# Loading the first chunk's later weight columns in four pieces, and spreading T4 between the bank sums, in a fused GeGLU kernel

One core of a Trainium2 chip. The metric is the device time of one execution in microseconds (us), as the median over executions; the profile's span is about 1.8 us shorter than the time of the same run.

## The reference

```python
B, S, D, F = 1, 2048, 1024, 3584          # all bf16
def reference(x, w_gate, w_up, w_down):
    return (gelu_tanh(x @ w_gate) * (x @ w_up)) @ w_down
```

## The kernel before

The rows of x are taken in two halves of 1024, each as two token blocks of 512. The products with gate (j = 0) and up (j = 1) go by pairs of 128-column blocks, four blocks (two pairs) to a chunk of weights. From the second pair on a pair is computed with seven products of half size in place of eight (the Strassen-Winograd scheme): sums S1 to S4 of weight blocks (fp32r, by GpSimd, here called POOL, or VectorE, DVE) and sums T1 to T4 of blocks of x (by VectorE) are multiplied, and the partial results are summed in the PSUM banks. The T sums of x are made once, the S sums for every pair. The first pair is done plainly, since nothing is ready yet, and the second is where the scheme starts: it needs all of x, all T sums and its own S sums at once. The change touches only this start.

The loads, in program order:

```python
for kd in range(KH, KD):                       # KD = 8 blocks of D, KH = 4
    load_xT(xT, 0, 0, kd, kd + 1)              # transposing load on SyncE
    if kd == KH + 1:
        for j in range(2):
            load_w(first, j, 5, KD, act, 0, FA)    # last rows of the first columns
for j in range(2):
    load_w(first, j, 0, KD, sp, FA, FG)        # the later columns (second pair)
for k0 in range(0, KD, KH):
    load_xT(xT, 0, 1, k0, k0 + KH)             # x of the second token block
new_chunk((0, 1))
for j in range(2):
    load_w((0, 1), j, 0, KD)
```

The second pair, from the sums on (cuts marked):

```python
for j in range(2):                 # in the main part, after the first pair
    s_sum(0, first_pair, j, "s1")  # on GpSimd
    s_sum(0, first_pair, j, "s3")
s_sum(0, first_pair, 0, "s2", True)   # True: on VectorE
s_sum(0, first_pair, 0, "s4", True)
t_sum("t1")
pair_quads(hT, 0, first_pair, (0, PPG), {}, 0)   # m1 and m2 of the second pair
# ... a22, b22 on ScalarE; s2 of j = 1, t2 on VectorE
# ... first pair for the second token block, with t3 in it
s_sum(0, first_pair, 1, "s4", True)
t_sum("t4", 0, KH // 2)

# in pair_quads, after m5 and m6:
for j in range(2):
    add_m5(QB[j], QB[j])           # bank sums Q0, Q1
    prep(j, "s2")
done("m5")                         # here: late_t4, the second half of T4
for j in range(2):
    mm(RB[j], j, s(j, "s3"), tsum["t3"], False)   # m7
    add_m5(V_[j], RB[j])           # bank sums V0, V1
    # ... gelu, mult
# ... m3 with S4, m4 with T4

def late_t4():
    t_sum("t4", KH // 2, KH)
    last_on["t4"] = last_on["dve"]
def late_s():                      # the third pair's sums, on GpSimd
    last_on["pool_wait"] = last_on["t4"]   # ... wait for the last piece of T4
    for name in S_NAMES:           # s1, s2, s3, s4, a22
        for j in range(2):
            s_sum(0, PPG, j, name)
then = {"m5": [late_t4], "m4": [late_s]}
```

In the third pair the products follow as m1, m5 of j = 0, m6, m5 of j = 1, m7, m3, m4 (in the pairs after it m6 comes ahead of m5); m2 of a pair comes after m1 of the next. m5 reads S1 and T1, m6 S2 and T2, m7 S3 and T3, m3 S4. "Third pair" and "fourth pair" below count from one.

## Time and profile before

| | before |
|---|---|
| time, median of 6 runs | 541.53 us (541.3 to 541.9, and one run of 3140 us that the median counts; 541.34 without it) |
| span of the profiled run | 539.7 us |
| TensorE busy | 534.5 us |
| TensorE stops up to 33 us, by distance of starts | 1.53 us |
| TensorE starts the third pair / the fourth pair's first fp32r product | 33.80 / 47.91 us |

How to read it: once the fourth pair has started, TensorE never waits again in this profile, so the start of the fourth pair tells what the first 48 us cost. Lines of the profile are from the timeline (start, length, engine, line, operation, tiles, shapes, count; PE is TensorE's matmuls, PEld its weight loads).

```profile
33.80 1.90 PE L389 MATMUL bank<-xT,w_mem 128*128 128x512 bf16 x8
...
39.04 2.30 POOL L360 TENSOR_TENSOR s_mem<-w_mem,s_mem 128x512 fp32r<-128x512 bf16 x2
...
47.91 2.42 PE L389 MATMUL bank<-t_mem,s_mem 128*128 128x512 f32 x9
```

The second line is the two S4 of the third pair, over at 41.34; the weight load that reads the second of them (the 29th of the 40 products from 35.35) starts at 41.69, so GpSimd has 0.35 us to spare there.

### The profile page before, as it was taken

The numbers are of one execution on the slowest core, as the hardware profiler recorded it, in microseconds if no ns is written. First come the engines' busy times: TensorE is split into PE (matmuls) and PEld (weight loads), VectorE is DVE, ScalarE is ACT, GpSimd is POOL, SyncE is SP. The second block draws the span as 40 slices with busy tenths as digits, with TensorE's granted clock in tenths as the row PEclk, the third lists the DMA queues.
The fourth block names the chain that finished last, engine by engine and source line by source line (L and its number), as shares of the span: only waits on it lengthen the run. The fifth ranks groups of instructions, "written<-read, shape, count | busy, mean of one in ns | idle before, by whom it ended". The sixth has DMA issues, their size and how long they took to land.

```text
span 539.7 us, 7117 instructions
## 1 busy us (share of the span) xinstructions
PE 534.5 (99%) x2384; PEld 377.1 (70%) x2384; DVE 362.2 (67%) x475; ACT 263.3 (49%) x446; POOL 239.5 (44%) x210
## 2 busy tenths in 40 slices
PE   8999999999999999999999999999999999999997
PEld 3577777666776676767776677777777766866865
DVE  0978777787875997889574434444444469969951
ACT  1555555555555319216465555555555551452270
POOL 1369877777776000000056776666777730000000
PEclk9999999999999999999999999999999999999999
DMA  9927687695827876789950404041331466677846
GB/s 231 310 84 215 203 247 227 198 274 185 286 77 252 296 244 223 257 265 314 319 187 1 156 1 157 9 147 55 102 110 48 157 199 218 229 242 242 288 147 209
DMA packets 84772, 102.70 MB, mean 190 GB/s; under 512 B 18688, under 2 KB 66304, under 8 KB 84736
## 3 DMA queue, kind: packets, MB, share of 16 engines
q1 hardware_dynamic: 61936, 80.30, 46.2%
q10 hardware_dynamic: 22800, 21.96, 13.2%
q8 instruction: 19, 0.31, 0.2%
q14 instruction: 17, 0.14, 0.1%
HBM read 85.98 MB, written 12.58 MB: 183 GB/s over the span
## 4 chain that ended last, share of the span: by engine, by line
PE 93%; SPq 2%; DVE 1%; issue 1%; DMA 1%; ACT 0%; ACTq 0%; DVEq 0%
PE bank L389 61%; PE bank L664 33%; SPq L172 2%; DMA xT<-in_x_dram 1%; SPq L161 0%; DVE hT L277 0%; DVE t_mem L245 0%; DVE bank L412 0%; DVE s_mem L358 0%; DVE t_mem L239 0%; ACT o_sb L717 0%; SPq L167 0%; ACTq L717 0%; DVEq L239 0%
## 5 line engine op out<-in xcount | busy, mean ns | idle before, releaser
L389 PE MATMUL bank<-t_mem,s_mem 128*128 128x512 f32 x1056 | 249.7, 394 | 0.2 <-DVE bank L412 0.2
L389 PEld LDWEIGHTS bank<-t_mem,s_mem 128*128 128x128 f32 x1056 | 198.2, 188 | 44.3 <-DVE bank L412 0.9
L360 POOL TENSOR_TENSOR s_mem<-w_mem 128x512 fp32r<-128x512 bf16 x104 | 121.9, 1195 | 196.8 <-DVE t_mem L245 116.2
L277 DVE TENSOR_TENSOR hT<-w_mem,bank 128x512 bf16<-128x512 f32 x104 | 71.2, 686 | 86.6 <-PE bank L389 46.2
L664 PE MATMUL bank<-t_mem,s_mem 128*128 128x512 f32 x544 | 127.2, 392 | 0.0
L664 PEld LDWEIGHTS bank<-t_mem,s_mem 128*128 128x128 f32 x544 | 102.1, 188 | 22.2
L412 DVE TENSOR_TENSOR bank<-bank,m 128x512 f32<-128x512 f32 x108 | 69.8, 693 | 44.9 <-ACT m L434 42.7
L389 PE MATMUL bank<-xT,w_mem 128*128 128x512 bf16 x432 | 98.1, 380 | 0.2 <-DMA w_mem<-in_w_up_dram 0.2
L272 ACT ACTIVATE w_mem<-bank 128x512 f32<-128x512 f32 x104 | 61.8, 596 | 54.0 <-DVE bank L412 36.3
L389 PEld LDWEIGHTS <-w_mem 128*128 128x128 bf16 x432 | 40.1, 98 | 52.1 <-issue 6.8
L574 DVE TENSOR_TENSOR t_mem<-w_mem 128x1024 fp32r<-128x1024 bf16 x56 | 65.6, 1217 | 0.0
L360 POOL TENSOR_TENSOR s_mem<-w_mem,s_mem 128x512 fp32r<-128x512 bf16 x50 | 62.2, 1268 | 0.0
L360 POOL TENSOR_TENSOR s_mem<-s_mem,w_mem 128x512 fp32r<-128x512 f32 x50 | 58.0, 1180 | 0.0
L439 ACT COPY bank<-bank 128x512 f32<-128x512 f32 x54 | 30.8, 570 | 39.0 <-PE bank L389 38.5
L373 ACT CAST s_mem<-w_mem 128x512 fp32r<-128x512 bf16 x54 | 33.0, 615 | 30.5 <-PE bank L389 29.2
L639 DVE TENSOR_TENSOR s_mem<-hT 128x512 fp32r<-128x512 bf16 x52 | 34.2, 685 | 10.2 <-PE bank L664 9.4
L434 ACT COPY m<-bank 128x512 f32<-128x512 f32 x54 | 31.7, 587 | 18.4 <-PE bank L389 18.3
L664 PEld LDWEIGHTS <-hT 128*128 128x128 bf16 x224 | 21.2, 98 | 26.7 <-issue 2.1
L444 ACT COPY bank<-bank 128x512 f32<-128x512 f32 x54 | 30.8, 570 | 12.8 <-PE bank L389 12.8
L717 ACT CAST o_sb<-bank 128x512 bf16<-128x512 f32 x28 | 15.3, 585 | 39.6 <-PE bank L664 39.6
L599 DVE TENSOR_TENSOR o_sb<-wd_sb,o_sb 128x512 fp32r<-128x512 bf16 x28 | 31.4, 1121 | 0.5
L571 ACT CAST t_mem<-w_mem 128x1024 fp32r<-128x1024 bf16 x28 | 26.9, 1047 | 0.0
(44 smaller groups left out, 235.7 us busy)
## 6 DMA issues: line engine op xcount, KB each, us to landing
t_mem<-t_dram SPq DMA_DIRECT2D x56, 512.0 KB, 5.4
w_mem<-in_w_gate_dram ACTq DMA_DIRECT2D x10, 1024.0 KB, 5.6
w_mem<-in_w_up_dram ACTq DMA_DIRECT2D x10, 1024.0 KB, 8.7
wd_sb<-in_w_down_dram SPq DMA_DIRECT2D x28, 256.0 KB, 5.0
t_dram<-o_sb SPq DMA_DIRECT2D x28, 256.0 KB, 2.4
wd_sb<-in_w_down_dram SPq DMA_DIRECT2D x12, 512.0 KB, 8.4
w_mem<-in_w_down_dram SPq DMA_DIRECT2D x10, 512.0 KB, 5.8
w_mem<-in_w_down_dram SPq DMA_DIRECT2D x4, 1024.0 KB, 6.3
```

Of the source, the lines that this page charges most:

```text
L272: act(nc.scalar.activation(out=g_sb, in_=ps[:], func=ACT.Gelu_apprx_tanh))
L277: nc.vector.tensor_tensor(out=hT[:, fc, tb * TB : (tb + 1) * TB], in0=g_sb, in1=ps[:], op=ALU.mult,)
L360: pool(nc.gpsimd.tensor_tensor(out=t, in0=in0, in1=in1, op=op))
L373: act(nc.scalar.copy(out=t, in_=a(1, 1)))
L389: nc.tensor.matmul(banks[bank][:], lhsT=lhs[:, c, :], rhs=rhs[:, c, :], start=start and c == 0, stop=c == KH - 1, skip_group_check=True,)
L412: nc.vector.tensor_tensor(out=banks[dst][:], in0=banks[src][:], in1=m5[j][:], op=ALU.add)
L434: act(nc.scalar.copy(out=m5[j][:], in_=banks[V_[j]][:]))
L439: act(nc.scalar.copy(out=banks[RB[j]][:], in_=banks[QB[j]][:]))
L574: dve(nc.vector.tensor_tensor(out=t, in0=in0, in1=in1, op=ALU.subtract))
L599: dve(nc.vector.tensor_tensor(out=t, in0=in0, in1=in1, op=ALU.subtract))
L639: dve(nc.vector.tensor_tensor(out=t, in0=in0, in1=in1, op=op))
L664: nc.tensor.matmul(banks[bset[u]][:], lhsT=lhs(i, u), rhs=rhs(i), start=start and i == 0, stop=stop and i == NS - 1, skip_group_check=True,)
```

## The change

Its intent is to take away each of TensorE's stops in the start: up's last rows no longer wait in ScalarE's queue, the second pair's first products need only half the rows of the later columns, GpSimd has one sum less ahead of T1, and V0 no longer stands behind half of T4. The diff, whole but for context lines:

```diff
-                load_w(first, j, 5, KD, act, 0, FA)
-    for j in range(2):
-        load_w(first, j, 0, KD, sp, FA, FG)
+                load_w(first, j, 5, KD, (act, sp)[j], 0, FA)
+    for k0 in range(0, KD, KH):
+        for j in range(2):
+            load_w(first, j, k0, k0 + KH, sp, FA, FG)
@@ in pair_quads
         for j in range(2):
             add_m5(QB[j], QB[j])
+            done(f"q{j}")
             prep(j, "s2")
         done("m5")
         for j in range(2):
             mm(RB[j], j, s(j, "s3"), tsum["t3"], False)
             add_m5(V_[j], RB[j])
+            done(f"v{j}")
@@ main part
-            for j in range(2):
-                s_sum(0, first_pair, j, "s1")
-                s_sum(0, first_pair, j, "s3")
+            for j, name in ((0, "s3"), (0, "s1"), (1, "s1")):
+                s_sum(0, first_pair, j, name)
@@
             t_sum("t2")
+            s_sum(0, first_pair, 1, "s3", True)
@@
+            t_sum("t4", 0, KH // 2)
             s_sum(0, first_pair, 1, "s4", True)
-            t_sum("t4", 0, KH // 2)
@@
-                def late_t4():
-                    t_sum("t4", KH // 2, KH)
+                def late_t4(c):
+                    t_sum("t4", c, c + 1)
                     last_on["t4"] = last_on["dve"]
@@
-                then = {"m5": [late_t4], "m4": [late_s]}
+                then = {
+                    "q0": [lambda: late_t4(KH - 2)],
+                    "v0": [lambda: late_t4(KH - 1)],
+                    "m4": [late_s],
+                }
```

## The prediction

> **What bounds the kernel now.** I read the page first, then the chain of work that ended last in order of time, then the timeline of the first 50 us, because the diff touches nothing later than the second pair of column blocks. From the page:
>
> ```profile
> PE 534.5 (99%) x2384; PEld 377.1 (70%) x2384; DVE 362.2 (67%) x475; ACT 263.3 (49%) x446; POOL 239.5 (44%) x210
> ```
>
> TensorE is idle 539.7 - 534.5 = 5.2 us of the whole span. The chain says where that can be won:
>
> ```profile
> 8.78 5.40 SPq L172
> ...
> 14.22 4.28 DMA xT<-in_x_dram
> ...
> 21.52 1.02 DVE t_mem L239
> ...
> 27.72 0.83 DVE t_mem L245
> ...
> 31.19 0.62 DVE bank L412
> 31.85 152.82 PE bank L389 x680
> 184.68 87.89 PE bank L664 x392
> ```
>
> From 31.85 us on, the end is set by an unbroken run of matmuls: 152.82 us for 680 is 0.225 us each. Before that the chain is loads of x, then VectorE (DVE). So whatever the change is worth must be won before about 37 us, as an earlier start of that run. TensorE's stops in that stretch, in the timeline (columns: start, length, engine, line, in brackets the idle time and what ended it):
>
> ```profile
> 11.13 2.33 PE L253 MATMUL bank<-xT,w_mem 128*128 128x512 bf16 x10 [0.15 <-DMA w_mem<-in_w_up_dram]
> ...
> 14.54 2.76 PE L389 MATMUL bank<-xT,w_mem 128*128 128x512 bf16 x12 [0.21 <-DMA w_mem<-in_w_up_dram]
> ...
> 31.85 2.10 PE L389 MATMUL bank<-t_mem,s_mem 128*128 128x512 f32 x8 [0.21 <-DVE bank L412]
> ```
>
> The bracket understates a stop, since a matmul's end is drawn about 0.16 us after the next one may start. By the distance between starts, less the usual 0.216 (bf16) or 0.227 (fp32r), I count: 0.25 at 8.66 (ScalarE's copy of the fourth block of x), 0.31 at 11.13 (last rows of up), 0.37 at 14.54 (later columns of up), 0.11 at 29.5 (bank sum Q0) and 0.49 at 31.85 (bank sum V0, which stood behind the second half of T4; 0.11 of it is seen at the step after). Together 1.53 us, 0.28% of 541.72. This is the ceiling.
>
> **What the Trainium skill says.** "SBUF — State Buffer", Who interferes with whom: a VectorE instruction with two SBUF inputs contends with a GpSimd instruction that reads SBUF, and whichever starts first holds the shared port for the whole instruction. The trace agrees, and I use it below:
>
> ```profile
> 12.78 5.38 POOL L360 TENSOR_TENSOR s_mem<-w_mem 128x512 fp32r<-128x512 bf16 x4 [11.48 <-DMA w_mem<-in_w_gate_dram]
> ...
> 15.63 1.52 DVE L358 TENSOR_TENSOR s_mem<-w_mem,s_mem 128x512 fp32r<-128x512 bf16 x1
> ...
> 17.07 3.24 DVE L236 TENSOR_TENSOR t_mem<-xT,xT 128x2048 fp32r<-128x2048 bf16 x1
> ```
>
> S4 takes 0.68 us at 27.04 with GpSimd idle, but 1.52 here; T1 takes 3.24, where T2 and T3 of the same size take 2.28. GpSimd's last two of the four take 1.60 each instead of 1.15. The two alternate, whole instructions at a time: T1 issued at 17.07 could only begin when GpSimd ended at 18.16. Operations on banks (L412, L277) have one SBUF input and show no such stretch (0.69).
> "DMA: Bandwidth & Descriptors", Issuing engines are not separate DMA queues: moving an issue to another engine saves sequencer time alone. The trace qualifies it: ScalarE issues gate's last rows at 4.49 and up's only at 7.46, since that issue's semaphore is reused and waits for an earlier load (landed 7.44); SyncE is at 4.84 at the same place of the program. And the ScalarE copy behind it waits as well.
>
> **The change, part by part.**
> *Last rows of up on SyncE.* Issued at about 4.84 instead of 7.46, landed about 9.3 (gate's took 4.5 us) instead of 11.09. The 0.31 stop goes. ScalarE no longer stands at that issue, so its copy at 8.03 can go at about 7.0: the 0.25 stop goes. The sixth and seventh x blocks are issued about 0.8 later (land near 10.0 and 10.7 instead of 9.46 and 9.95); TensorE wants them at about 11.0 and 11.9. TensorE is 0.56 ahead at the end of the first units.
> *Four pieces by halves of D.* 512 KB landed in 14.49 - 12.71 = 1.78 us, so each 256 KB piece is 0.89: with the queue starting 0.5 later I estimate gate-a 11.8, up-a 12.7, gate-b 13.6, up-b 14.5. The product at 14.54 needs only up-a, so its 0.37 goes: TensorE is 0.93 ahead. But the bytes are the same and the DMA engines are full from 9.5 to 18, so the transposed x of the second token block lands where it did, at about 16.5. TensorE used it at 17.14 and would now want it at 16.2: it stops 0.35 there, and 0.6 remains.
> *Three sums on GpSimd instead of four, one more on VectorE.* S3 starts at 11.8, S1 at 13.6 (gate-b), the other S1 at 14.75, over at 15.9. VectorE: S2 waits for the port until 15.85, done 16.45; S4 alone, 17.05; T1 2.2, done 19.3, against 20.32 before: 1.05 ahead. The added S3 costs 0.6 (step of S2 and S4 alone). Left: 0.45 ahead. Q0 starts at 28.3 instead of 28.78.
> *T4 by single blocks.* Before: Q0, Q1, T4 half (1.13 step), V0, V1. After: Q0, T4 block (0.6), Q1, V0, T4 block, V1. Steps of 0.6 from 28.3: Q0 done 29.0, Q1 30.2, V0 30.8, last T4 block 31.35, V1 32.0. TensorE takes Q0's bank at 29.05 (0.1 stop), Q1's at 30.2 (0.1), V0's at 31.1 without a stop, V1's at 32.05. The pair's last product ends its issue at 33.0 instead of 33.80: 0.8 ahead here.
>
> **What takes it back.** GpSimd's sums for the next chunk wait for the last piece of T4, and these four lines show how tight that is:
>
> ```profile
> 29.98 1.21 DVE L245 TENSOR_TENSOR t_mem<-xT,t_mem 128x1024 fp32r<-128x1024 bf16 x1
> ...
> 31.42 2.28 POOL L360 TENSOR_TENSOR s_mem<-w_mem 128x512 fp32r<-128x512 bf16 x2 [13.26 <-DVE t_mem L245]
> ...
> 33.66 2.73 POOL L360 TENSOR_TENSOR s_mem<-s_mem,w_mem 128x512 fp32r<-128x512 f32 x2
> ...
> 35.35 9.44 PE L389 MATMUL bank<-t_mem,s_mem 128*128 128x512 f32 x40
> ```
>
> The second S2 ends at 33.66 + 2.73 = 36.39, and the product that reads it (four fp32r matmuls after 35.35) starts at 36.46: it has no slack. GpSimd needs 36.39 - 31.19 = 5.2 us from the end of T4 to that S2. So TensorE's 0.8 can be kept only as far as T4 ends before 31.19. I find 31.35: VectorE's 0.45 ahead is spent on V0 (0.6), which now stands before the last block. TensorE then stops about 0.8 to 1.0 us inside the third pair, before m6, and the balance is 0.15 us worse. Further: VectorE's staging step at 34.67 (0.70), which took the port between GpSimd's two S2 and stretched the second to 1.6, comes up to 0.8 earlier. If it enters one sum earlier, the next step gets in before the second S2 too: another 0.6. I give this one chance in four, so +0.15 again on the mean. Against it stand the landings: if gate-b lands 0.4 earlier than I put it, T4 ends 0.4 earlier and so does everything after. Sum: near 0, from +0.3 to -0.2. I choose -0.1: 541.6.
>
> **Rivals.**
> (a) All stops are removed and kept, -1.2 to -1.5 us: 540.4. For it: each stop has a part of the change aimed at it. Against it: the 0.07 us slack of the second S2, and x at 16.5.
> (b) The gain is carried in part: VectorE is more than 0.6 ahead, because the loads land earlier (the DMA engines moved only 227 GB/s from 6 to 9 us, 282 after), T4 ends at 30.7: -0.5, 541.2.
> (c) The port goes against it: two staging steps before the second S2, or a late landing of the second x half: +0.8, 542.5.
> (d) Two more issues on SyncE delay x past 17.2, with a new stop of up to 1 us at the first unit of the second token block. SyncE spent 5.40 us on that issue, which reads to me as waiting for room and would absorb the 1.2 us of added issues. I put this low.
>
> **Range and chances.** Ceiling -1.5 (540.2), bad end about +1.0 (542.7); two fast runs of the kernel before differ by 0.4. So 541.6, and 8 in 10 for 540.7 to 542.6. 2% is 10.8 us, seven times the ceiling and ten times the worst wait I can name: within 2% is 0.98, and 0.01 on each side.
>
> **What would show it.** Right: no stop at 8.7, 11.1 and 14.5; T1 near 2.3 us; one S3 on VectorE; V0 no longer awaited; POOL's first sum of the next chunk at 31.1 to 31.7, and a new TensorE wait for POOL, 0.5 to 1 us, near 35 to 36. Wrong: POOL starting before 31.0 (then rival b), no wait for POOL at all (rival a), T1 waiting for x after 17.3 (rival d). A time outside the range would mean a wait in this stretch that I haven't seen, as nothing after 50 us is edited.

## The result, and the profile after

542.04 us as the median of 6 runs (541.79 to 544.4), against 541.53 us. Ratios here are the mean time of one kernel's runs over that of the other's of the same rounds, so not quite the ratio of the medians quoted: 1.0019, 95% interval 1.0000 to 1.0039. Executions over 1.5% slower than the fastest of the same kernel are left out of the means. The class is "same". Two of the six (544.4 and 543.1) pull the mean up; the profile shows a smaller step, a span of 540.0 against 539.7.

The chain of waits of the changed kernel, where before there was VectorE between 18.5 and 31.8:

```profile
10.41 6.88 DMA xT<-in_x_dram
17.29 0.04 issue
17.33 7.07 PE bank L254 x32
24.40 160.46 PE bank L390 x712
184.85 87.89 PE bank L667 x392
```

The loads and x are followed by matmuls alone, from 17.33 us on. Yet the first down projection starts at 184.85 where it was 184.68: TensorE is 0.17 later, not earlier. The timeline of the changed kernel shows where it gains and loses:

```profile
12.84 3.62 PE L390 MATMUL bank<-xT,w_mem 128*128 128x512 bf16 x16
...
17.31 2.29 DVE L237 TENSOR_TENSOR t_mem<-xT,xT 128x2048 fp32r<-128x2048 bf16 x1 [0.24 <-DMA xT<-in_x_dram]
17.33 7.07 PE L254 MATMUL bank<-xT,w_mem 128*128 128x512 bf16 x32 [0.88 <-DMA xT<-in_x_dram]
...
31.06 0.68 DVE L246 TENSOR_TENSOR t_mem<-xT,t_mem 128x512 fp32r<-128x512 bf16 x1
...
31.97 2.29 POOL L361 TENSOR_TENSOR s_mem<-w_mem 128x512 fp32r<-128x512 bf16 x2 [15.45 <-PE bank L390]
...
33.46 1.90 PE L390 MATMUL bank<-xT,w_mem 128*128 128x512 bf16 x8
...
39.60 2.29 POOL L361 TENSOR_TENSOR s_mem<-w_mem,s_mem 128x512 fp32r<-128x512 bf16 x2
...
40.82 0.75 PEld L390 LDWEIGHTS bank<-t_mem,s_mem 128*128 128x128 f32 x4 [0.34 <-POOL s_mem L361]
...
41.95 2.59 PEld L390 LDWEIGHTS bank<-t_mem,s_mem 128*128 128x128 f32 x12 [0.37 <-POOL s_mem L361]
...
48.09 2.19 PE L390 MATMUL bank<-t_mem,s_mem 128*128 128x512 f32 x8
```

Line by line. The sixteen products of the second pair run without the stop at 14.54: this part works. Then TensorE stops for x of the second token block, which landed at 17.29 (16.51 before): 1.04 us by the distance of starts. T1 takes 2.29 instead of 3.24, and V0 is not awaited, so the third pair starts at 33.46, 0.34 ahead of before. But the last block of T4 ends at 31.74 (31.19 before), GpSimd starts at 31.97 (31.42), ends its second S4 at 41.89 (41.34), and TensorE waits for both S4. (The profile puts GpSimd's start down to TensorE, whose matmul ended at 31.80; T4's last block ended at 31.74, and GpSimd starts 0.23 us after T4's end in both kernels, so it is the T4 that it waits for.)

So the third pair takes 48.09 - 33.46 = 14.63 us, where it took 47.91 - 33.80 = 14.11: 0.52 us lost there, 0.34 gained ahead of it, 0.18 worse. This difference is the measure that I use below: the start of the third pair tells what loads and VectorE did, the length of the third pair whether TensorE waited for GpSimd (14.11 to 14.13 is a third pair without waits in every run). The length is counted from the third pair's first product to the fourth pair's first fp32r product, 64 products later.

Where x lost 0.8 us is seen in the windows view (window, length, then busy us and count of PE, PEld, DVE, ACT, POOL; clock; DMA share; GB/s). First the kernel before, then the changed one:

```profile
14.00:14.50 0.50, 0.33 (x2) 0.00 (x0) 0.50 (x2) 0.14 (x1) 0.50 (x1) 1.00 1.13 189
14.50:15.00 0.50, 0.46 (x3) 0.23 (x4) 0.50 (x2) 0.43 (x1) 0.50 (x1) 1.00 1.27 289
```

```profile
14.00:14.50 0.50, 0.50 (x4) 0.21 (x3) 0.31 (x1) 0.47 (x1) 0.50 (x1) 1.00 0.78 78
14.50:15.00 0.50, 0.50 (x5) 0.20 (x3) 0.18 (x1) 0.24 (x1) 0.29 (x1) 1.00 0.25 39
```

The DMA engines move 78 and 39 GB/s for a whole microsecond, in the middle of a queue that has x waiting. The transposing load of x was issued at 10.41, and its issue was over at 14.95; the last of the four pieces landed at 15.17. A few 512-byte packets of that piece were still starting up to 14.75 (in the kernel before, up to 14.0), one after another, while little else moved. In every run of this case that issue ended 0.2 to 0.4 us before the landing of the last plain piece ahead of it in SyncE's queue, and in all eleven traces with both loads in that one queue x landed 2.0 to 2.3 us after that piece (14.49 and 16.51 before, 15.17 and 17.29 after).

### The profile page after: what moved, and what is told of

It reads as the page before. It is cut to its first block, busy times and chain, and to the rows that moved or that the text cites. A ratio compares the mean times of both kernels' runs of the same rounds, so it can differ in the third digit from the quotient of the medians.

```text
span 540.0 us, 7123 instructions
## 1 busy us (share of the span) xinstructions
PE 534.5 (99%) x2384; PEld 377.4 (70%) x2384; DVE 362.8 (67%) x477; ACT 263.8 (49%) x446; POOL 237.4 (44%) x209
## 4 chain that ended last, share of the span: by engine, by line
PE 96%; DMA 2%; SPq 1%; ACT 0%; ACTq 0%; issue 0%
PE bank L390 62%; PE bank L667 33%; PE bank L254 1%; DMA xT<-in_x_dram 1%; DMA w_mem<-in_x_dram 1%; SPq L172 0%; SPq L161 0%; ACT o_sb L720 0%; ACTq L161 0%; ACTq L720 0%
## 5 line engine op out<-in xcount | busy, mean ns | idle before, releaser
L361 POOL TENSOR_TENSOR s_mem<-w_mem 128x512 fp32r<-128x512 bf16 x103 | 119.3, 1178 | 199.1 <-DMA w_mem<-in_w_up_dram 103.5
```

The source lines that it names most:

```text
L361: pool(nc.gpsimd.tensor_tensor(out=t, in0=in0, in1=in1, op=op))
```

## The experiments

Eleven runs were made, of ten kernels (e12 is e9's kernel again), all with correct results. e1 to e4 ran on one chip, e6 to e9 on a second, e10 to e12 on a third. The traces of e1 to e4 lack 36 of the 2384 matmul records, so a count such as x7 below is not a missing product. Times are medians; "before" is the kernel before in the same rounds on the same chip. The landing times of single loads and the ends of T and S sums are from the traces ("GpSimd starts" is its first sum for the third pair, "fourth pair starts" its first fp32r product):

| run | time (before) us | ratio, 95% interval | x landed | T1 ends | last T4 ends | GpSimd starts / second S4 ends | third pair starts | it takes | fourth pair starts |
|---|---|---|---|---|---|---|---|---|---|
| before | 541.53 | | 16.51 | 20.32 | 31.19 | 31.42 / 41.35 | 33.80 | 14.11 | 47.91 |
| the change | 542.04 (541.53) | 1.0019 (1.0000 to 1.0039) | 17.29 | 19.60 | 31.74 | 31.97 / 41.90 | 33.46 | 14.63 | 48.09 |
| e1 loads only | 543.65 (541.64) | 1.0030 (1.0006 to 1.0053) | 16.99 | 21.73 | 32.60 | 32.83 / 42.78 | 35.24 | 14.13 | 49.37 |
| e2 sums only | 541.63 (541.64) | 1.0002 (0.9972 to 1.0031) | 16.52 | 19.38 | 31.52 | 31.75 / 41.72 | 33.27 | 14.64 | 47.91 |
| e3 up only | 542.05 (541.64) | 0.9997 (0.9971 to 1.0023) | 16.74 | 20.28 | 31.15 | 31.39 / 41.33 | 33.78 | 14.12 | 47.90 |
| e4 pieces only | 542.77 (541.64) | 1.0016 (0.9991 to 1.0041) | 16.58 | 21.30 | 32.16 | 32.40 / 42.33 | 34.78 | 14.11 | 48.89 |
| e6 halves on ScalarE | 544.46 (541.71) | 1.0056 (1.0037 to 1.0076) | 18.61 | 21.79 | 33.93 | 34.16 / 44.09 | 35.65 | 14.64 | 50.29 |
| e7 early GpSimd | 541.71 (541.71) | 1.0006 (0.9992 to 1.0021) | 17.26 | 20.18 | 32.46 | 30.75 / 41.14 | 34.16 | 14.11 | 48.27 |
| e8 both | 544.50 (541.71) | 1.0052 (1.0032 to 1.0071) | 19.32 | 22.48 | 35.54 | 33.83 / 44.20 | 37.74 | 14.11 | 51.85 |
| e9 sums, early GpSimd | 541.67 (541.71) | 1.0003 (0.9987 to 1.0019) | 16.36 | 19.46 | 31.76 | 30.04 / 40.42 | 33.48 | 14.12 | 47.60 |
| e10 before, early GpSimd | 541.52 (541.57) | 0.9999 (0.9985 to 1.0013) | 16.21 | 20.01 | 31.02 | 28.78 / 39.70 | 33.66 | 14.13 | 47.79 |
| e11 three pieces | 541.08 (541.57) | 0.9991 (0.9979 to 1.0004) | 15.89 | 19.14 | 31.41 | 29.70 / 40.11 | 33.10 | 14.12 | 47.22 |
| e12 as e9, again | 541.17 (541.57) | 0.9999 (0.9985 to 1.0013) | 16.06 | 19.16 | 31.45 | 29.73 / 40.14 | 33.13 | 14.11 | 47.24 |

The timed ratios can't separate steps of 0.1 us to 0.5 us (0.02% to 0.1%): nearly all intervals hold 1. The arguments rest on where the traces put things. They have a limit too: in e7 gate's first later piece landed at 12.65, in the changed kernel at 11.63, with the same loads. A difference in place of under 0.3 us between two single traces isn't read as an effect, unless a later sum explains it step by step.

The times also carry something that no edit touches. In three of the profiled runs TensorE stopped in the down projection for a load of t_mem from t_dram: 0.45 us in e3, 1.4 us in two stops in e4, and 0.9 us in e7 (by distance of starts):

```profile
246.85 1.38 PE L667 MATMUL bank<-t_mem,s_mem 128*128 128x512 f32 x5 [0.64 <-DMA t_mem<-t_dram]
```

The traces of the kernel before and of the change have no such stop. So the place of the fourth pair, and not the time or the span, is compared below.

### The two halves of the change, and the two halves of its loads: e1 to e4

e1 undoes all edits to sums and T4, e2 all edits to loads. e3 and e4 each put one edit of the loads on the kernel before:

```diff
# e3_up_only
-                load_w(first, j, 5, KD, act, 0, FA)
+                load_w(first, j, 5, KD, (act, sp)[j], 0, FA)
# e4_pieces_only
-    for j in range(2):
-        load_w(first, j, 0, KD, sp, FA, FG)
+    for k0 in range(0, KD, KH):
+        for j in range(2):
+            load_w(first, j, k0, k0 + KH, sp, FA, FG)
```

> The loads of the change alone (up's last rows on SyncE, four pieces), sums and T4 as before. Theory (issue): x of the second token block comes late because its issue on SyncE stands behind three more pieces of work, at 10.4 us instead of 8.8; so it lands at 17.2 to 17.4 here too, with a TensorE stop of about 1.0 us there, and no stops at 8.7, 11.1, 14.5. Rival (sums): the late x has to do with the changed order of sums on GpSimd and VectorE; then it lands at 16.5 here. Time: T4 ends near 31.2 to 31.6 as GpSimd again has four sums and T1 shares the port; 541.5 to 542.0.

> The sums and T4 order of the change alone, loads as before. Theory: x lands at 16.5 and the stops at 8.7, 11.1, 14.5 stay; T1 takes about 2.3 us and ends near 19.3; the stop for V0 at 31.85 goes, but the last T4 block ends at 31.3 to 31.5 (before 31.19), GpSimd starts 0.1 to 0.3 later than before, and the gain of 0.5 us at V0 is lost at the products of the third pair that read S4: final place of TensorE within 0.15 us of before, 541.4 to 541.7. Rival (V0 was the bound): TensorE keeps 0.4 us or more, 541.1.

> Only up's last rows on SyncE. Theory (issue): x's issue starts 0.6 later than in the kernel before (9.4), x lands 0.2 to 0.4 later (16.7 to 16.9); stops at 8.7 and 11.1 go, 14.5 stays or grows; later TensorE is given back the gain at V0, as VectorE's T4 doesn't move: 541.4 to 541.7. Rival: x lands at 16.5 unmoved, since the engines carry the same bytes.

> Only the four pieces. Theory (issue): x's issue starts 1.0 later (9.8), x lands at 16.9 to 17.2; the stop at 14.5 goes, those at 8.7 and 11.1 stay; little or no stop at x as TensorE is only 0.37 ahead: 541.4 to 541.8. Rival: x lands at 16.5 unmoved.

**e2** did what its theory said. The third pair starts at 33.27, 0.53 ahead of before; GpSimd starts 0.33 later; the third pair takes 14.64; the fourth pair starts at 47.91, not a hundredth from before:

```profile
30.84 0.68 DVE L245 TENSOR_TENSOR t_mem<-xT,t_mem 128x512 fp32r<-128x512 bf16 x1
...
31.75 2.30 POOL L360 TENSOR_TENSOR s_mem<-w_mem 128x512 fp32r<-128x512 bf16 x2 [15.85 <-PE bank L389]
...
33.27 1.90 PE L389 MATMUL bank<-xT,w_mem 128*128 128x512 bf16 x7
...
47.91 1.27 PE L389 MATMUL bank<-t_mem,s_mem 128*128 128x512 f32 x4
```

**e1** was expected at 541.5 to 542.0 and took 543.65; the fourth pair starts 1.46 later than before. I had counted T1's wait for the port, and not what makes GpSimd start:

```profile
14.19 5.39 POOL L361 TENSOR_TENSOR s_mem<-w_mem 128x512 fp32r<-128x512 bf16 x4 [12.88 <-DMA w_mem<-in_w_gate_dram]
...
18.49 3.24 DVE L237 TENSOR_TENSOR t_mem<-xT,xT 128x2048 fp32r<-128x2048 bf16 x1
```

S1, GpSimd's first sum in the old order, adds columns over all rows of gate. In four pieces, up's first half stands ahead of gate's second half, which lands at 14.05 where the whole of gate landed at 12.71. All four sums move by 1.4 us, and T1 with them (it ends at 21.73, 20.32 before). The change's own order, S3 first, is what hides this: S3 needs the first halves alone (11.70 in the changed kernel). **e4** shows the same without up's move: GpSimd starts at 13.76, the fourth pair 0.98 later. So the pieces can't be taken without the new order of sums, and my range for e4 (541.4 to 541.8) was wrong for the same reason as e1's.

**e3** fits in its trace, not in its time (542.05, for 541.4 to 541.7; part of that is the late stop named above): the stops at 8.7 and 11.1 go, x lands 0.23 later, TensorE waits longer at 14.50 (0.70 of idle time instead of 0.21), and the fourth pair starts at 47.90. Alone, it is worth nothing.

On x, e1 answers against its rival: with the old sums x lands at 16.99, late, though short of the 17.2 to 17.4 expected. But the theory "a later issue lands later" is weak: in e4 the issue starts 0.95 us later than before (9.73 against 8.78) and x lands at 16.58, as before. e3 and e4 move x by 0.23 and 0.07, both together by 0.48 (e1), 0.78 (the change) and 0.75 (e7). What orders the traces is not x's issue, which started anywhere from 8.71 to 10.72, but the last plain piece, 2.0 to 2.3 us ahead of x: it landed at 14.46 in e3 and e4, 14.81 in e1, 15.17 in the change and 15.23 in e7. In e1 and the change one of the four pieces came 1.50 and 1.61 us after the one ahead of it (gate's second half, up's second half), the other second halves 0.76 to 1.14; in e7 gate's first half came 2.2 us after the block of x ahead of it, 0.9 in the change. Why one piece dragged in each is not shown.

### Where could x be had earlier: e6 and e8

The second halves go to ScalarE, behind its copy of x, so that SyncE comes to x after two pieces. e8 adds the earlier release of GpSimd that is shown with e7 below:

```diff
-    for k0 in range(0, KD, KH):
-        for j in range(2):
-            load_w(first, j, k0, k0 + KH, sp, FA, FG)
+    for j in range(2):
+        load_w(first, j, 0, KH, sp, FA, FG)
@@ in first_units, behind transpose_x0(1)
+                for jj in range(2):
+                    load_w(first, jj, KH, KD, act, FA, FG)
```

> The changed kernel, with the second halves of gate's and up's later columns issued by ScalarE after its copy of x, so that SyncE comes to the second token block's x after two pieces and not four. Theory (x late): in the changed kernel the x issue has to wait for the last piece (issue over at 14.95, last piece landed at 15.17, DMA engines nearly idle from 14.0 to 15.0); here x lands at 16.0 to 16.7 instead of 17.29 and the stop of 1.04 us at 17.33 shrinks to 0.5 or less. T1 then starts at 16.7 to 17.1, T4 ends 0.3 to 0.6 earlier, so GpSimd starts at 31.4 to 31.7, and the fourth pair's first fp32r product starts at 47.5 to 47.8 (48.09 in the changed kernel, 47.91 before). Rival (same bytes, same end): x lands at 17.2 or later here too.

> Both of the former two. Theory: they add: x at 16.0 to 16.7, GpSimd from about 29.7, no wait for GpSimd; the fourth pair starts at 46.9 to 47.3, 0.6 to 1.0 ahead of the kernel before: 540.6 to 541.0, ratio 0.998 to 0.999. Rival: VectorE, which has no idle time from T1 to V1, keeps it at 47.5.

Both missed, by 2 us and more. In e6 x was issued at 9.53, ahead of up's second half (10.01), and landed after it. What waited for that half:

```profile
18.47 1.04 PE L391 MATMUL bank<-xT,w_mem 128*128 128x512 bf16 x4 [2.33 <-DMA w_mem<-in_w_up_dram]
18.49 1.15 POOL L362 TENSOR_TENSOR s_mem<-w_mem 128x512 fp32r<-128x512 bf16 x1 [3.98 <-DMA w_mem<-in_w_up_dram]
```

In e6 up's second half, 256 KB on ScalarE's queue at 10.01, landed at 18.43: 8.4 us, where such a piece took 3.5 to 5.3 in SyncE's queue, and gate's second half, on ScalarE's queue at 8.91, took 4.2. x, on the other queue at the same time, took 9.1 us from the start of its issue and landed at 18.61. In e8 the two landed at 19.11 and 19.32. From 16 to 18 us of e6 the DMA engines counted as busy and moved only 183 and 117 GB/s. So in these two traces a plain load and a transposing load side by side, on two queues, held each other up: x landed 4.7 and 5.1 us after the last plain piece ahead of it in its own queue, for 2.0 to 2.3 elsewhere. No run varies this alone. What held e6's theory up to here, the issue ending just before the landing of the last piece ahead in the queue, showed once more (13.69 and 13.87).

e8's 51.85 is not all the loads'. From one of TensorE's starts to the next 3.4 us passed there (2.7 in e6), and from about 19.4 to 22.8 us its granted clock was down to 0.50, with bf16 products 0.43 us apart instead of 0.216. By the distances this cost 1.7 us (window, columns as above):

```profile
20.00:21.00 1.00, 1.00 (x3) 0.30 (x2) 1.00 (x1) 0.07 (x1) 0.33 (x1) 0.50 0.91 169
```

Two of e6's four executions and three of e8's have a mean clock of 0.996 or 0.997 instead of 1.0, so their medians may hold the same; e6's profiled run does not.

### Is it GpSimd's start that takes the gain: e7, e9, e10, e12

The wait on T4 is for the port, not for data; here GpSimd waits for the T4 block behind Q0 instead of the one behind V0 (still a piece of T4, no data wait is taken away):

```diff
                 def late_t4(c):
                     t_sum("t4", c, c + 1)
-                    last_on["t4"] = last_on["dve"]
+                    if c == KH - 2:
+                        last_on["t4"] = last_on["dve"]
```

e7 is this on the changed kernel; e9 and e12 are this on e2 (sums only); e10 is the kernel before, with GpSimd waiting for T4's first half:

```diff
             t_sum("t4", 0, KH // 2)
+            last_on["t4"] = last_on["dve"]
@@
                 def late_t4():
                     t_sum("t4", KH // 2, KH)
-                    last_on["t4"] = last_on["dve"]
```

> The changed kernel, with GpSimd's first sums of the next chunk waiting for the T4 block behind Q0 instead of the one behind V0. Theory (GpSimd sets the end): GpSimd starts at 30.1 to 30.3 instead of 31.97, shares the port with the last T4 block, and finishes the second S4 at 40.6 to 41.0 instead of 41.90; TensorE's waits at the third pair's S4 products go and the fourth pair starts at 47.5 to 47.7 instead of 48.09, or 541.6. Rival (TensorE's end is set by V0/V1 and x): the fourth pair still starts at 48.0 to 48.1, GpSimd's lead being given back through VectorE's wait for the port. The x lands at 17.0 to 17.4 again if its lateness isn't chance.

> The kernel before with the sums and T4 order of the change (as in the run of sums only) and GpSimd waiting for the T4 block behind Q0. Theory (GpSimd sets the end): sums only started the fourth pair at 47.91 just as before, because GpSimd's second S4 ended at 41.72; here it ends at 40.5 to 40.9 and the fourth pair starts at 47.3 to 47.5: 541.1 to 541.3. Rival: 47.9 again.

> The kernel before, with GpSimd's first sums of the next chunk waiting for the first half of T4 instead of the second. If the kernel before is bound by VectorE's V0 behind T4 and GpSimd has slack there (its second S4 ended at 41.35, read at 41.9), an earlier GpSimd gains nothing: the fourth pair starts at 47.9 or, as GpSimd's sums now take the port from T4's second half, up to 0.8 later: 47.9 to 48.7. Rival (GpSimd sets the end in the kernel before too): 47.4 to 47.6.

> The same kernel as sums with the early release, once more with more rounds, as its trace is 0.3 us ahead of the kernel before and three rounds couldn't show it: the fourth pair starts at 47.5 to 47.7 again, and the ratio to the kernel before is 0.9985 to 1.0000 with x and loads landing as before.

In **e9** and **e12** GpSimd starts at 30.04 and 29.73, and the third pair takes 14.12 and 14.11: no wait for GpSimd is left. e9, to be laid beside e2's lines:

```profile
30.04 2.74 POOL L360 TENSOR_TENSOR s_mem<-w_mem 128x512 fp32r<-128x512 bf16 x2 [14.05 <-DVE t_mem L245]
...
30.92 0.84 DVE L245 TENSOR_TENSOR t_mem<-xT,t_mem 128x512 fp32r<-128x512 bf16 x1
...
33.48 1.90 PE L389 MATMUL bank<-xT,w_mem 128*128 128x512 bf16 x8
...
47.60 1.73 PE L389 MATMUL bank<-t_mem,s_mem 128*128 128x512 f32 x6
```

GpSimd's sums now share the port with the last T4 block (0.84 instead of 0.68, and GpSimd's two take 2.74 instead of 2.30), which costs V1 and TensorE 0.21 (33.48 against 33.27). The 0.52 of the third pair is won: 47.60, 0.31 ahead of before, if 0.1 short of the 47.3 to 47.5 expected. e12 repeats it at 47.24, ahead of its 47.5 to 47.7, but its loads were earlier too (gate 12.24 against 12.54 in e9). **e7** shows the same in the length of the third pair, 14.11. Its expected 47.5 to 47.7 was missed, at 48.27, as three of its four pieces came 0.8 to 1.0 later than in the changed kernel: gate's second half at 14.37 instead of 13.56, so that S2 and S4 came late on VectorE and T1 started at 17.89. That is the spread of loads, not of the edit.

**e10** is the counter-test. In the kernel before, GpSimd had 0.35 us to spare, so starting it early should win nothing, and it doesn't:

```profile
28.78 3.26 POOL L360 TENSOR_TENSOR s_mem<-w_mem 128x512 fp32r<-128x512 bf16 x2 [10.92 <-DVE t_mem L245]
...
31.68 2.14 PE L389 MATMUL bank<-t_mem,s_mem 128*128 128x512 f32 x8 [0.34 <-DVE bank L412]
```

T4's second half takes 1.36 instead of 1.21, V0 is awaited longer (0.34 of idle time instead of 0.21), and the third pair takes 14.13 as before. The fourth pair starts at 47.79, 0.1 ahead of the range expected and 0.2 behind the rival's, 0.55 behind e12 on the same chip, 0.15 of which the gate loads explain (12.39 against 12.24). So the bound moved: VectorE's V0 in the kernel before, GpSimd's start in the changed one.

### A version without the pieces' price: e11

e9's edits, with gate whole and first, and only up in two pieces:

```diff
-    for j in range(2):
-        load_w(first, j, 0, KD, sp, FA, FG)
+    load_w(first, 0, 0, KD, sp, FA, FG)
+    for k0 in range(0, KD, KH):
+        load_w(first, 1, k0, k0 + KH, sp, FA, FG)
```

> Sums and T4 of the change, the early release of GpSimd, and only up's later columns in two pieces by halves (gate's whole, and first). The stop at 14.5 should go without delaying gate's last row, on which the first S1 waits: gate lands at 12.5 to 12.8, up's first half at 13.5 to 13.8, x at 16.4 to 16.7 (one more issue on SyncE). As VectorE has no idle time from T1 to V1, the 0.4 us gained at 14.5 should be taken back at the bank sums: the fourth pair starts at 47.4 to 47.7, no better than without the pieces (47.60). Rival: it keeps the 0.4 us, 47.2.

x landed at 15.89, the stop at 14.5 is gone, and TensorE reached the second token block at 16.10, 0.5 ahead of e12 on the same chip. It kept none of it:

```profile
28.94 4.33 PE L390 MATMUL bank<-t_mem,s_mem 128*128 128x512 f32 x16 [0.29 <-DVE bank L413]
...
33.10 1.90 PE L390 MATMUL bank<-xT,w_mem 128*128 128x512 bf16 x8
```

It stops for Q0 at 28.94, and the third pair starts at 33.10 against 33.13. VectorE works without a break from T1 to V1, and T1 started at 16.85 against 16.88, since it stands behind S2 and S4, and that S2 (1.62 instead of 0.68) waited until GpSimd's last sum was over at 15.66. Its fourth pair starts at 47.22, below my 47.4 to 47.7, by as much as the chip's loads were early (gate 12.21). Of all runs it has the best median, 541.08 us, 0.5 below the kernel before in the same rounds; the interval of its ratio (0.9979 to 1.0004) still holds 1, and so does that of e12 (541.17). They are the candidates to beat both kernels, ahead by 0.7 us in place, of which about 0.3 is the edits' and the rest the loads' of that chip; more isn't shown.

## Why the prediction was right, and where not

The time, 542.04, lay in the range (540.7 to 542.6), the class was "same", and the balance near zero was right for the main reason given: V0's gain is lost to GpSimd, which starts the next sums behind a T4 that ends later. The sign was not right: the forecast was -0.1, the trace shows +0.18 and the medians +0.5. And that the 0.18 lies near the "0.15 us worse" of the working is partly luck: T4 ended 0.55 later than before where 0.16 was forecast, and 0.35 us of room at the second S4, which the prediction didn't see, took up most of the difference. Step by step:

- *Stops at 8.7, 11.1 and 14.5.* Right; none is left, and TensorE was 0.84 ahead at 13.70, for 0.93 predicted.
- *x at about 16.5, a stop of 0.35.* Wrong, and this is rival (d), which I put low: x landed at 17.29, and the stop was 1.04 us. The step that failed is "the bytes are the same and the DMA engines are full from 9.5 to 18": they were nearly empty from 14.0 to 15.0, while the last piece dragged on ahead of x. I had read the 5.40 us of the issue as room that absorbs added issues. In its place the runs show x tied to the landing of the last plain piece, 2.0 to 2.3 us behind it, and that piece at 15.17 instead of the forecast 14.5. Up to gate's second half (13.56 for 13.6) the forecast of the pieces held. Why the last one dragged is open.
- *T1 done at 19.3, 1.05 ahead.* It ended at 19.60, 0.72 ahead, by x's lateness; its length (2.29) and S3's on VectorE (0.68) were as said. In e2, where x was in time, T1 ended at 19.38.
- *Q0 at 28.3, last T4 block at 31.35.* 28.66 and 31.74. The mechanism and the size of each step held (V0's 0.6 against VectorE's lead); the term that was too favourable is the lead at Q0, 0.12 instead of 0.45, again by x. e2, with x in time, had its last T4 block at 31.52.
- *TensorE 0.8 ahead at the end of the second pair.* 0.34. Lateness of x is not all of it: e2, with x in time, had 0.53.
- *"The second S2 has no slack", a wait of 0.8 to 1.0 before m6.* Wrong in place. In the third pair m5 of j = 0 comes first, so that the product at 36.46 read the first S2; the second S2 had about 0.8 us to spare. What had least to spare was the second S4, in m3 (0.35 before). After the change there is a small wait at m6 (0.23 of weight-load idle time at 37.00), and the main ones are at 40.82 and 41.95; the third pair is 0.52 us longer altogether. Had I laid the order of products beside GpSimd's ends for all S, not for S2 alone, I would have had this. The sum could still come out near, since the same queue of GpSimd sums feeds all of them.
- *The staging step taking the port one sum earlier.* It came 0.33 earlier (34.34), waited for the port, and stretched one sum (1.62) before the second S2 ended, as before. The further 0.6 didn't come.

The rest of the difference in time is not this change's as far as the traces show: in the profiled runs the changed kernel is 0.17 us later at 184 us and at 536 us alike, while the medians differ by 0.5 us and the means by 1.0, with two long runs (543.1 and 544.4) among the six. No trace of those two exists; a late load of t_mem, as in e3, e4 and e7, would fit, and is not shown for them.

## What to carry to other kernels

When a wait is removed from the engine that sets the end, follow the work that the moved instructions feed: here T4 left V0's way, and GpSimd, released by T4's last piece, took back the 0.5 us one pair later. Measure a stage by its own length (third pair, 14.11 or 14.63), not only by the total, if loads shift everything by as much as the effect. And cut a load in pieces only together with the order of its readers: a sum that reads across the pieces waits for the last of them (e1 and e4, 1.4 and 1.0 us).

## What the Trainium skill lacked or had wrong

- "DMA: Bandwidth & Descriptors", Issuing engines are not separate DMA queues, says that loads started by several engines interleave and that this saves sequencer time only. It doesn't say that it can cost. In e6 and e8 a plain 256 KB piece on ScalarE's queue beside a transposing load on SyncE's took 8.4 and 9.2 us instead of 3.5 to 5.3, and the transposing load landed 1.3 us and 2.0 us later than in the changed kernel.
- No page that I found says that SyncE's issue of a large transposing load stays occupied until 0.2 to 0.4 us before the landing of the plain load ahead of it in the queue (14.18 and 14.49 before, 14.95 and 15.17 after, 13.69 and 13.87 in e6), or that its data then lands 2.0 to 2.3 us after that one.
- "SBUF — State Buffer", Who interferes with whom: the exclusive lock fits the traces here. It doesn't say who is next when both have work waiting: here an engine that waits gets in at the end of the other's instruction even if the other has more ready, so GpSimd and VectorE alternate (sums of 1.60 and 1.62 instead of 1.15, S4 on VectorE 1.52 instead of 0.68).
- "TensorE: Matmul & The Clock Gate", Back-to-back issue gap, gives about 131 ns for each matmul of N=512 in a stream with weight loads. Here 32 bf16 matmuls with their weight loads take 7.07 us, 216 ns between starts (the page's figure for an isolated one), and fp32r 227 ns.
